# The gate behind the second dense weights, multiplied on TensorE instead of VectorE

## The chip, the core and the metric

The kernel runs on one core of a Trainium2 chip. The metric is the device time of one execution in microseconds (us); the kernel before has a median of 937.81 us in three runs (935.88 to 937.83).

## What is computed

Three layers follow one another. The first is a linear attention with a decaying state, over 4 sequences of 768 tokens and 8 heads of 48. Its output, 3072 rows of 384, goes through a dense layer (384 to 2048 and back) and then through a layer of 8 experts, in which each token goes to one expert by its logits, 384 tokens to each.

```python
for t in range(S):                                   # attention
    cur = np.einsum('bhd,bhe->bhde', u[None] * kt, vt)
    y[:, :, t] = np.einsum('bhd,bhde->bhe', rt, state + cur)
    state = wt[:, :, :, None] * state + np.einsum('bhd,bhe->bhde', kt, vt)

h = x @ w_in                                         # dense layer
g = h * (1.0 / (1.0 + np.exp(-1.702 * h)))
x = g @ w_out

logits = x @ w_gate                                  # experts: best (token, expert) pairs first
h = np.maximum(x[mask] @ w1[e], 0.0)
out[mask] = h @ w2[e]
```

For a block of tokens the logits are `(g @ w_out) @ w_gate`, which is also `g @ (w_out @ w_gate)`. The product of the two weights, 2048 x 8, is what this change is about.

## The kernel before

The 3072 tokens are cut into 8 blocks of 384 (`NB`), and the 2048 inner columns of the dense layer into 16 groups of 128 (`NFS`, index f). All weights and activations are held as a high and a low float32r part, so that a product takes three matmuls: high by high, high by low, low by high. `Ffn.g1` (line 1001) makes a group of g for a block in nine matmuls of 384 columns; `Ffn.part` (line 1029) multiplies it by the output weights into three accumulators of 128 tokens (`acc`).

The weights of the dense layer come as 64-bit numbers in 16 chunks, by turns one of `w_in` (two groups f) and one of `w_out` (two groups f). `split64` turns each into its two parts with steps on ScalarE, VectorE and GpSimd; the last step of a chunk is line 699, after which the plan sets `wdone[("in", i)]` or `wdone[("out", i)]`. `rhs2(f, part)` is the 128 x 384 piece of the output weights for group f. Meanwhile 24 `unit`s compute the attention, three for a block, with VectorE, GpSimd, ScalarE and small TensorE products.

The order of instructions on each engine is written by a small planner, `Issue` (line 60), when the program is built. It keeps a planned time `t` of TensorE and the planned time to which each other engine is busy. Chains (Python generators) are added with a rank; `pump` advances every chain whose time has come, lower ranks first. A step that yields `("T", d)` moves TensorE's time by d. `until(cond)` lets planned time go on in steps of 0.1 us until the condition holds, and issues in each step one `spin`: a matmul of the identity by itself (line 638), which computes nothing that is used. Three PSUM banks named `s1` are shared by the chains (`bank`).

The main loop runs over `seq`: half of block 0, block 1, the rest of block 0, then blocks 2 to 7, a g1 and, two places later, its g2. After a block's last g2 its rows x2 are stored, and `logits` (line 1073) multiplies them by the gate on VectorE, eight products with a sum for each 128 tokens.

The last block has no time for that, so its logits are made from g itself: `thin_logits` multiplies g by `wogp`, the high and low part of `wog` = `w_out @ w_gate`. `wog` is made by `wog_steps`, a chain of rank 5, the last rank. It starts when `gate_weights` has loaded the gate, spread over all partitions (`wgB`), after the last output chunk is split. For each f GpSimd adds the two parts of the weights (line 1137), and VectorE makes for each of the 8 experts a product with a sum along the row (line 1141, into `wog[:, f, e]`). At its end `todo[1] = 1` is set. Before the last block's first g1 the main loop waits for two things:

```python
if blk not in ffn:
    sc.until(lambda: xdone.get(blk) == NU)
    if blk == NBLK - 1:
        sc.until(lambda: todo[1])
```

After the last block come the router (eight rounds of a search on the logits) and the experts.

Of the kernel before, what the change touches and what calls it, by code (L numbers as in the profile page):

```python
# [8 lines left out]
F32 = mybir.dt.float32  # L9
F32R = mybir.dt.float32r  # L10
# [5 lines left out]
AF = mybir.ActivationFunctionType  # L16
OP = mybir.AluOpType
# [19 lines left out]
def dram(ap, off, dims):  # L37
    return bass.AP(tensor=ap.tensor, offset=ap.offset + off, ap=dims)
# [427 lines left out]
def kernel(ctx, tc, r, k, v, w, rk, u, us, w_in, w_out, w_gate, w1, w2, out):  # L466
    nc = tc.nc
    V, A, P, T = nc.vector, nc.scalar, nc.gpsimd, nc.tensor
    H, D = u.shape
    B, NC = r.shape[:2]  # L470
    Dm = H * D
# [3 lines left out]
    E, NC3 = w1.shape[:2]  # L475
# [3 lines left out]
    KT = Dm // 128  # L479
# [8 lines left out]
    NCVA, NCVB, NCVC = 3, 2, 3  # L488
# [18 lines left out]
    consts = ctx.enter_context(tc.tile_pool(name="consts", bufs=1))  # L507
# [6 lines left out]
    s1p = st1.enter_context(tc.tile_pool(name="s1p", bufs=1))  # L514
# [4 lines left out]
    sc = Issue()  # L519
    sc.nc = nc  # L520
    R = {n: Ring(m) for n, m in (("s1", 3), ("g1", 2), ("Q", 1), ("Fw", 1), ("At", 1),
                                 ("kn", 1), ("y", 1), ("g", 2), ("gh", 3), ("cva", NCVA), ("cvb", NCVB), ("cvc", NCVC),
                                 ("xa", 1), ("xb", 1), ("wk", 32), ("hold", NHOLD))}

    def wait(*names):
        while not all(R[n].ok() for n in names):
            yield 0.1

    def bank(shape=(128, 512)):
        yield from wait("s1")  # L530
        i = R["s1"].new()
        return psum.tile(list(shape), F32, name="s1", bufs=3), lambda: R["s1"].free(i)
# [82 lines left out]
    ident = consts.tile([128, 128], F32, name="ident")  # L615
    dif = cv.tile([128, 128], F32, name="cva", bufs=NCVA)
    P.iota(dif, pattern=[[1, 128]], base=0, channel_multiplier=-1, allow_small_or_imprecise_dtypes=True)
    V.tensor_scalar(ident, dif, 0.0, None, op0=OP.is_equal)  # L618
    later = s1p.tile([128, 128], U8, name="later")
    V.tensor_scalar(later, dif, 0.0, None, op0=OP.is_gt)  # L620
    lead = s1p.tile([R2, HP * PW + 1], U8, name="lead")
# [20 lines left out]
    Whi, Wlo, Wring, wdone = {}, {}, {}, set()  # L642
# [68 lines left out]
    def rhs2(f, part):  # L711
        return (Whi, Wlo)[part]["out", f // 2][:, (f % 2) * Dm:(f % 2 + 1) * Dm]
# [358 lines left out]
    wgB, scr = [], []  # L1071
# [57 lines left out]
    wog = consts.tile([128, NFS, E], F32, name="wog")  # L1129
    wogp = consts.tile([128, NFS * 2 * E + 128], F32R, name="wogp")  # L1130

    def wog_steps():
        while not wgB:
            yield 0.5
        for f in range(NFS):
            a = scr[0][:, 1]
            P.tensor_tensor(a, rhs2(f, 0).bitcast(F32), rhs2(f, 1).bitcast(F32), op=OP.add)  # L1137
            yield (("P", 1.0),)
            for e in range(E):
                yield from sc.room("V", 0.4)  # L1140
                V.scalar_tensor_tensor(scr[0][:, 0], a, 1.0,  # L1141
                                       wgB[e // 4][:, (e % 4) * Dm:(e % 4 + 1) * Dm],
                                       op0=OP.mult, op1=OP.mult, accum_out=wog[:, f, e:e + 1])
                yield (("V", 0.47),)
        hi, lo = (wogp[:, :NFS * 2 * E].rearrange("p (f x e) -> p f x e", f=NFS, x=2)[:, :, x]
                  for x in range(2))
        A.activation(hi, wog, AF.Copy)
        V.tensor_tensor(lo, wog, hi.bitcast(F32), op=OP.subtract)
        todo[1] = 1
# [52 lines left out]
    def thin_logits(f, ps):  # L1202
# [3 lines left out]
        for i in range(2):  # L1206
# [4 lines left out]
    start = [begin[un // NU] - LEAD[min(un // NU, 3)] + PACE[min(un // NU, 3)] * (un % NU)  # L1211
             for un in range(NUNIT)]
    slot = [-1]
    split64()
    for un in range(NUNIT):
        sc.add(unit(un) if un < NU else paced(un), 1 if un < NU else URANK)
    sc.add(gate_weights(), 3)
    sc.add(wog_steps(), 5)
    sc.add(get_part(), 2)
    sc.spin = spin  # L1220
    sc.until(lambda: xdone.get(0) == NU)
    ffn = {}
    for s in range(len(seq) + 2):
# [4 lines left out]
        if s < len(seq):  # L1228
            blk, f = seq[s]
# [13 lines left out]
        else:  # L1243
            if f2 == 0:
                last = ffn[b2]
                g_ = bank()
                try:
                    next(g_)
                except StopIteration as e:
                    ps, done = e.value  # L1250
# [188 lines left out]
    for s in range(E * NF3 + 2):  # L1439
        at[0] = s  # L1440
        i, f = divmod(s, NF3)
# [72 lines left out]
```

## Time and profile before

| | |
|---|---|
| median of 3 runs | 937.81 us |
| the profiled execution: time, span from first to last instruction | 941.33 us, 939.6 us |
| TensorE matmuls busy | 882.1 us (94%) |
| TensorE weight loads busy | 834.0 us (89%) |
| VectorE busy | 682.2 us (73%) |
| ScalarE busy | 350.9 us (37%) |
| GpSimd busy | 314.0 us (33%) |
| mean granted TensorE clock | 0.947 |

In the rows PE is TensorE's matmuls, PEld its weight loads, DVE VectorE, ACT ScalarE, POOL GpSimd. L1141 is line 1141. PEclk is the share of the full TensorE clock that was granted. A busy share says that an engine executes something, and not that the result is used: the spins of line 638 count as busy. Some of the time in which TensorE waits is therefore seen as spins and some as idle time.

### The profile page before, as it was taken

The numbers are of one execution on the slowest core, as the hardware profiler recorded it, in microseconds if no ns is written. First come the engines' busy times: TensorE is split into PE (matmuls) and PEld (weight loads), VectorE is DVE, ScalarE is ACT, GpSimd is POOL, SyncE is SP. The second block draws the span as 40 slices with busy tenths as digits, with TensorE's granted clock in tenths as the row PEclk, the third lists the DMA queues.
The fourth block names the chain that finished last, engine by engine and source line by source line (L and its number), as shares of the span: only waits on it lengthen the run. The fifth ranks groups of instructions, "written<-read, shape, count | busy, mean of one in ns | idle before, by whom it ended". The sixth has DMA issues, their size and how long they took to land.

```text
span 939.6 us, 18095 instructions
## 1 busy us (share of the span) xinstructions
PE 882.1 (94%) x6867; PEld 834.0 (89%) x6867; DVE 682.2 (73%) x1791; ACT 350.9 (37%) x632; POOL 314.0 (33%) x319
## 2 busy tenths in 40 slices
PE   6977997999999999999999979989999989999995
PEld 5766996899999999999999979979889889899995
DVE  8699699799979789799797783666676776653210
ACT  1433553332333333333323034024554643657521
POOL 4477346512232324233223101021333423346311
PEclk8779999899999999999999999978898998899998
DMA  8526432423313222133210000058787977969900
GB/s 262 160 85 190 143 110 95 143 85 96 98 51 96 73 75 82 50 97 97 63 54 5 2 25 1 18 151 187 190 241 154 275 207 155 259 186 268 245 26 26
DMA packets 48504, 113.37 MB, mean 121 GB/s; under 512 B 7616, under 2 KB 13600, under 8 KB 48416
## 3 DMA queue, kind: packets, MB, share of 16 engines
q1 hardware_dynamic: 31680, 70.51, 23.8%
q0 software_dynamic: 12288, 34.61, 17.5%
q10 hardware_dynamic: 4448, 7.08, 2.2%
q8 instruction: 54, 0.88, 0.4%
q14 instruction: 34, 0.28, 0.1%
HBM read 75.95 MB, written 10.03 MB: 91 GB/s over the span
## 4 chain that ended last, share of the span: by engine, by line
PE 62%; DVE 20%; issue 9%; DMA 3%; POOL 2%; ACT 2%; ACTq 0%; DVEq 0%; POOLq 0%
PE g L1001 24%; PE acc L1029 22%; PE s L393 5%; DVE cvb L1078 3%; DVE cvb L1141 3%; PE s L920 2%; PE s L913 2%; DVE Q L765 2%; DVE gl L1053 2%; PE s L836 2%; DVE cvc L681 2%; PE acc L638 1%; DVE cvc L678 1%; PE s L453 1%; DMA hold<-in_w 1%
## 5 line engine op out<-in xcount | busy, mean ns | idle before, releaser
L1029 PE MATMUL acc<-wk,gh 128*128 128x384 f32 x1080 | 282.0, 341 | 0.3 <-ACT cva L1406 0.3
L1029 PEld LDWEIGHTS acc<-wk,gh 128*128 128x128 f32 x1080 | 196.5, 191 | 1.5 <-ACT cva L1406 0.6
L1029 PE MATMUL acc<-wk,gl 128*128 128x384 f32 x540 | 183.1, 339 | 0.0
L1001 PE MATMUL g<-xhb,wk 128*128 128x384 f32 x576 | 171.1, 350 | 11.0 <-DVE gl L1053 5.2
L1001 PE MATMUL g<-xha,wk 128*128 128x384 f32 x576 | 171.8, 350 | 6.9 <-DVE gl L1053 3.7
L1047 ACT ACTIVATE g<-g 128x384 f32<-128x384 f32 x128 | 60.8, 475 | 217.4 <-PE g L1001 195.4
L1001 PEld LDWEIGHTS g<-xhb,wk 128*128 128x128 f32 x576 | 108.8, 195 | 13.4 <-DVE gl L1053 5.6
L1001 PEld LDWEIGHTS g<-xha,wk 128*128 128x128 f32 x576 | 108.3, 193 | 10.7 <-DVE gl L1053 5.3
L1029 PEld LDWEIGHTS acc<-wk,gl 128*128 128x128 f32 x540 | 103.0, 191 | 0.0
L1001 PE MATMUL g<-xlb,wk 128*128 128x384 f32 x288 | 100.3, 348 | 0.0
L1001 PE MATMUL g<-xla,wk 128*128 128x384 f32 x288 | 99.4, 345 | 0.0
L1078 DVE SCALAR_TENSOR_TENSOR cvb<-cva,raw 128x384 f32<-128x384 f32 x168 | 95.6, 569 | 4.6 <-ACT cva L1117 1.5
L1053 DVE TENSOR_TENSOR gl<-g,gh 128x384 fp32r<-128x384 f32 x116 | 64.0, 551 | 39.3 <-ACT gh L1050 38.9
L1330 POOL DMA_DIRECT2D wk<-hold x64 | 57.6, 1045 | 85.3 <-ACT wk L1324 76.6
L1060 ACT ACTIVATE gh<-g 128x384 fp32r<-128x384 f32 x64 | 31.3, 489 | 129.0 <-PE g L1001 113.9
L1141 DVE SCALAR_TENSOR_TENSOR cvb<-cvb,raw 128x384 f32<-128x384 f32 x128 | 71.4, 557 | 10.8 <-POOL cvb L1137 5.1
L1063 DVE SCALAR_TENSOR_TENSOR gl<-g,gh 128x384 fp32r<-128x384 f32 x64 | 35.2, 552 | 60.7 <-ACT gh L1060 56.0
L793 POOL TENSOR_TENSOR S<-S,Q 48x192 f32<-48x192 f32 x40 | 49.4, 1235 | 88.6 <-DVE Q L765 87.1
L638 PE MATMUL acc<-ident 128*128 128x128 bf16 x842 | 60.1, 227 | 4.2 <-DVE ident L618 4.2
L638 PEld LDWEIGHTS <-ident 128*128 128x128 bf16 x842 | 51.4, 102 | 10.1 <-issue 5.1
L1050 ACT ACTIVATE gh<-g 128x384 fp32r<-128x384 f32 x116 | 56.9, 490 | 8.5 <-DVE cva L1112 3.2
L393 PEld LDWEIGHTS <-cvc 128*128 128x128 bf16 x840 | 53.3, 158 | 5.9 <-issue 2.6
(222 smaller groups left out, 1432.4 us busy)
## 6 DMA issues: line engine op xcount, KB each, us to landing
hold<-in_w SPq DMA_DIRECT2D x64, 384.0 KB
wk<-hold POOLq DMA_DIRECT2D x64, 384.0 KB
nat_m<-in_rk SPq DMA_DIRECT2D x20, 384.0 KB
raw<-in_w_in SPq DMA_DIRECT2D x8, 768.0 KB
raw<-in_w_out SPq DMA_DIRECT2D x8, 768.0 KB
nat_v<-in_v SPq DMA_DIRECT2D x22, 256.0 KB
nat_w<-in_w SPq DMA_DIRECT2D x22, 226.2 KB
nat_k<-in_k SPq DMA_DIRECT2D x22, 224.0 KB
```

The costliest lines, as they stand in the source:

```text
L393: nc.tensor.matmul(ps[:, :E], G[j], oh[:, j], start=(j == 0), stop=(j == NJ - 1))
L638: T.matmul(warm[0][:, Dm:], i16, i16, start=warm[1], stop=False, skip_group_check=True)
L793: P.tensor_tensor(h_, h_, Q[64 * s:64 * s + D, 1:HP * PW:PW, None].to_broadcast([D, HP, D]), op=OP.mult)
L1001: T.matmul(p, self.l1(kt, f, a), (self.xh, self.xl)[b_][:, kt], start=(kt == 0 and n == 0), stop=(kt == KT - 1 and n == 2))
L1029: T.matmul(self.acc[tt], gs[a][:, tt * C:(tt + 1) * C], self.r2(f, b_), start=(f in self.cuts and n == 0), stop=(end and n == 2))
L1047: A.activation(p, p, AF.Gelu_apprx_sigmoid)
L1050: A.activation(gh, p, AF.Copy)
L1053: V.tensor_tensor(gl, p, gh.bitcast(F32), op=OP.subtract)
L1063: V.scalar_tensor_tensor(gl, p, 0.0, gh.bitcast(F32), op0=OP.max, op1=OP.subtract)
L1078: V.scalar_tensor_tensor(scr[0][:, 0], x2, 1.0, wgB[e // 4][:, (e % 4) * Dm:(e % 4 + 1) * Dm], op0=OP.mult, op1=OP.mult, accum_out=router. ...
L1141: V.scalar_tensor_tensor(scr[0][:, 0], a, 1.0, wgB[e // 4][:, (e % 4) * Dm:(e % 4 + 1) * Dm], op0=OP.mult, op1=OP.mult, accum_out=wog[:, f ...
L1330: P.dma_start(out=Wlo[key].bitcast(F32), in_=raw, accum_op=OP.add)
```

## The change

`wog_steps` is written anew. It no longer waits for the whole of the gate on all partitions. When the first output chunk is split it loads the gate as 8 rows of 384 (`wg8`), and TensorE turns it into three pieces of 128 x 8 (`wgT`). Then, for each f, as soon as its output chunk is split: six matmuls, whose stationary operands are the 128 x 128 pieces of the high and the low weights and whose moving operand is a float32r identity (`identr`), give the transposed sum of the two parts in a PSUM bank; ScalarE copies it to `wT`; three matmuls, `wT` by `wgT`, give the 128 x 8 piece of `wog`, which ScalarE copies. `wT` has one buffer with a ring of its own. The rank stays 5, `todo[1]` is set at the end as before, and `wgB` is still loaded for `logits`. GpSimd's addition and VectorE's eight products per f are gone.

```diff
-                                 ("kn", 1), ("y", 1), ("g", 2), ("gh", 3), ("cva", NCVA), ("cvb", NCVB), ("cvc", NCVC),
+                                 ("kn", 1), ("y", 1), ("wT", 1), ("g", 2), ("gh", 3), ("cva", NCVA), ("cvb", NCVB), ("cvc", NCVC),
...
+    identr = s1p.tile([128, 128], F32R, name="identr")
+    V.tensor_scalar(identr, dif, 0.0, None, op0=OP.is_equal)
...
+    wg8 = consts.tile([E, Dm], F32, name="wg8")
+    wgT = consts.tile([128, KT, E], F32, name="wgT")
+
     def wog_steps():
-        while not wgB:
+
+        while ("out", 0) not in wdone:
             yield 0.5
+        nc.scalar.dma_start(wg8, dram(w_gate, 0, [[Dm, E], [1, Dm]]))
+        yield 3.0
+        ps, done = yield from bank()
+        for kt in range(KT):
+            T.transpose(ps[:, kt * E:(kt + 1) * E], wg8[:, kt * 128:(kt + 1) * 128], ident[:E, :E])
+        A.activation(wgT, ps[:, :KT * E].rearrange("p (k e) -> p k e", k=KT), AF.Copy)
+        done()
+        yield (("T", 0.2), ("A", 0.2))
         for f in range(NFS):
-            a = scr[0][:, 1]
-            P.tensor_tensor(a, rhs2(f, 0).bitcast(F32), rhs2(f, 1).bitcast(F32), op=OP.add)
-            yield (("P", 1.0),)
-            for e in range(E):
-                yield from sc.room("V", 0.4)
-                V.scalar_tensor_tensor(scr[0][:, 0], a, 1.0,
-                                       wgB[e // 4][:, (e % 4) * Dm:(e % 4 + 1) * Dm],
-                                       op0=OP.mult, op1=OP.mult, accum_out=wog[:, f, e:e + 1])
-                yield (("V", 0.47),)
+            while ("out", f // 2) not in wdone:
+                yield 0.5
+            yield from wait("wT")
+            ps, done = yield from bank()
+            for kt in range(KT):
+                for n in range(2):
+                    T.matmul(ps[:, kt * 128:(kt + 1) * 128], rhs2(f, n)[:, kt * 128:(kt + 1) * 128], identr,
+                             start=(n == 0), stop=(n == 1))
+            yield (("T", 0.9),)
+            yield from sc.room("A", 0.4)
+            i = R["wT"].new()
+            wT = s1p.tile([128, KT * 128], F32, name="wT")
+            A.activation(wT, ps[:, :KT * 128], AF.Copy)
+            done()
+            yield (("A", 0.5),)
+            ps, done = yield from bank()
+            for kt in range(KT):
+                T.matmul(ps[:, :E], wT[:, kt * 128:(kt + 1) * 128], wgT[:, kt], start=(kt == 0),
+                         stop=(kt == KT - 1))
+            R["wT"].free(i)
+            A.activation(wog[:, f], ps[:, :E], AF.Copy)
+            done()
+            yield (("T", 0.4), ("A", 0.2))
```

## Rows read from the trace of the kernel before

**Rows 1.** The page's first line.

```profile
span 939.6 us, 18095 instructions
```

**Rows 2.** Windows: stretch and its length, busy time (count) by engine, clock, DMA, GB/s.

```profile
45.00:103.00 58.00, 46.90 (x426) 42.76 (x425) 53.15 (x63) 22.19 (x38) 38.92 (x26) 0.88 0.42 132
103.00:150.00 47.00, 42.52 (x250) 40.58 (x248) 41.00 (x49) 23.99 (x42) 22.55 (x13) 1.00 0.37 120
150.00:172.20 22.20, 17.49 (x190) 16.37 (x190) 18.72 (x22) 4.71 (x7) 15.82 (x12) 0.77 0.41 125
172.20:519.80 347.60, 346.66 (x2505) 334.60 (x2501) 298.23 (x756) 115.46 (x242) 99.58 (x99) 1.00 0.25 75
519.80:538.00 18.20, 18.20 (x327) 18.20 (x327) 13.96 (x50) 0.00 (x0) 2.98 (x3) 1.00 0.01 2
538.00:549.80 11.80, 6.57 (x41) 6.25 (x38) 9.08 (x32) 1.86 (x5) 1.01 (x1) 0.99 0.01 1
549.80:552.80 3.00, 3.00 (x9) 3.00 (x10) 2.50 (x8) 1.47 (x4) 0.00 (x0) 0.50 0.37 131
```

The columns of busy time are PE, PEld, DVE, ACT and POOL, in this order.

**Rows 3.** Windows of line 638 (the spins): stretch, length, PE and PEld busy, clock, DMA.

```profile
45.00:103.00 58.00, 8.61 (x134) 7.59 (x134) 0.88 0.42 132
103.00:150.00 47.00, 0.00 (x0) 0.00 (x0) 1.00 0.37 120
150.00:172.20 22.20, 4.31 (x71) 4.05 (x71) 0.77 0.41 125
```

**Rows 4.** Waits of PE from 165 to 560 us: total, times, longest.

```profile
PE g L1001 <- DVE gl L1053: 5.4, 2, 5.2
```

**Rows 5.** Timeline around the last block's start: start, us, what, idle time before.

```profile
519.79 18.43 PE L638 MATMUL acc<-ident 128*128 128x128 bf16 x327
...
547.91 0.31 ACT L1147 ACTIVATE wogp<-wog 128x128 fp32r<-128x128 f32 x1 [28.49 <-DVE cvb L1141]
...
549.76 0.69 PE L1001 MATMUL g<-xhb,wk 128*128 128x384 f32 x1 [5.23 <-DVE gl L1053]
```

**Rows 6.** Groups from 165 to 560 us: busy us, mean ns of one, idle before.

```profile
L1141 DVE SCALAR_TENSOR_TENSOR cvb<-cvb,raw 128x384 f32<-128x384 f32 x128 | 71.4, 557 | 10.8 <-POOL cvb L1137 5.1 <-DMA raw<-in_w_gate 2.6
L1050 ACT ACTIVATE gh<-g 128x384 fp32r<-128x384 f32 x92 | 45.1, 490 | 7.5 <-DVE cva L1112 3.2 <-ACT cva L1117 2.4
L1141 DVE DVE_READ_ACCUMULATOR cvb<-cvb,raw 128x1 f32 x128 | 10.4, 81 | 0.0
```

**Rows 7.** Line 977 from 460 to 560 us: duration, first and last start.

```profile
L977 POOL TENSOR_TENSOR xlb<-y,xhb x3: 1014/1048/1271, 480.6 to 513.2; 128x384 fp32r<-128x384 f32 x3
```

**Rows 8.** Timeline of PE from 281 us on, at the full clock.

```profile
281.24 0.60 PE L855 MATMUL s<-ident,nat_k 112*128 112x112 f32 x4
281.62 0.59 PE L1029 MATMUL acc<-wk,gh 128*128 128x384 f32 x2
...
282.75 1.05 PE L913 MATMUL s<-nat_r,S 112*128 112x128 f32 x8
283.74 0.44 PE L920 MATMUL s<-At,nat_v 128*64 128x128 f32 x4
```

**Rows 9.** The chain that ended last, from 300 us on: one of nine matmuls.

```profile
303.74 1.56 PE acc L1029 x9
```

**Rows 10.** Windows of line 699: stretch, length, DVE and POOL busy (count), clock, DMA.

```profile
30.00:103.00 73.00, 2.09 (x2) 13.82 (x6) 0.86 0.44 136
103.00:150.00 47.00, 0.00 (x0) 10.60 (x5) 1.00 0.37 120
150.00:172.20 22.20, 1.68 (x1) 4.44 (x2) 0.77 0.41 125
```

**Rows 11.** Waits of DVE from 103 to 172 us: total, times, longest.

```profile
DVE gl L1053 <- ACT gh L1050: 3.0, 2, 1.8
```

**Rows 12.** The chain that ended last, from 160 us on: the gate's transfer.

```profile
168.29 5.03 DMA raw<-in_w_gate
```

## The prediction

> **What bounds the kernel now.** I read the profile in this order: the span and its shares, then the stretches, then what TensorE executes in each, then its waits. The profiled execution has a span of 939.6 us [rows 1]; the run around it took 941.33 us and the median of the runs shown is 937.81 us. So I sum on the span and take 1.8 us off at the end.
>
> The stretches [rows 2] show three regimes. From 172.2 to 519.8 us TensorE is busy 346.66 of 347.60 us at the full clock: it is the bound, and what VectorE does there costs nothing as long as TensorE doesn't wait for it. From 45 to 172.2 us TensorE is not full (46.90 of 58.00, 42.52 of 47.00, 17.49 of 22.20) and VectorE has about as much to do (53.15, 41.00, 18.72); this is the stage that splits the incoming weights. Then the busy share misleads: 519.8 to 538.0 us reads 18.20 of 18.20 busy, yet it is no work. The timeline [rows 5] shows 327 matmuls of line 638 there, 18.43 us from 519.79. Line 638 is `spin`, which multiplies the identity by itself while the plan waits. So a busy TensorE has to be corrected by the spins, which the windows of line 638 give [rows 3]: 8.61 us from 45 to 103, none from 103 to 150, 4.31 us from 150 to 172.2.
>
> What is waited for at 519.8 us is in the code: before the last block's first g1 the loop runs `sc.until(lambda: todo[1])`, and `todo[1]` is set at the end of `wog_steps`. The trace agrees: ScalarE's first step on `wog` starts at 547.91 us after 28.49 us of idleness that VectorE's line 1141 ended [rows 5]. The plan gave VectorE too little time per step, so TensorE, having spun, runs a little and then stands idle 5.23 us until 549.76 us for a `gl` that lies behind the rest of line 1141 in VectorE's queue [rows 5]. That one wait is 5.2 of the 5.4 us that the main loop's g1 waited for VectorE from 165 to 560 us [rows 4]. After the idle stretch it runs 3.00 us at a granted clock of 0.50 [rows 2], the lower of its two levels.
>
> **What the change removes.** 128 products on VectorE of 557 ns and 128 accumulator reads of 81 ns [rows 6], 82 us, with GpSimd's 16 additions ahead of them. In the TensorE-bound stretch that is worth nothing. Its worth lies at the end: spinning 519.79 to 538.03, 18.2 us; the idle 5.2 us; half of 3.0 us at the half clock, 1.5 us. Sum 24.9 us, if `todo[1]` is set before 519.8 and nothing else is late there. What is late next? The last block's x: its last piece (line 977, `xlb`) starts at 513.2 us and takes about 1 us [rows 7], 5.6 us ahead of the wait. Then TensorE is simply continuous.
>
> By the Trainium skill ("Trainium Kernel Development and Optimization", Best Practices) one should judge TensorE by MFU and by the busy share of LDWEIGHTS instead of matmul busy time. Here LDWEIGHTS is 18.20 of 18.20 us [rows 2] while nothing is computed, so the row decides against that rule.
>
> **What it adds.** Per f, six matmuls (three column groups, high and low part, moving `identr`), one ScalarE copy of 128x384, three products with `wgT` of eight columns, and a small ScalarE copy. The trace has no float32r matmul with 128 moving columns, so I bound it. A one-instruction transpose of 112 columns takes (281.62 - 281.24) / 4 = 0.095 us, a full-precision product (two instructions each) (283.74 - 282.75) / 8 = 0.124 us per instruction [rows 8]; float32r with 384 columns takes 1.56 / 9 = 0.173 us in one instruction [rows 9]. One instruction it will be, as there: I take 0.11, so 6 x 0.11 = 0.66 us; ends 6 x 0.095 = 0.57 and, if it went as two passes, 6 x 0.248 = 1.49 us. The three `wgT` products are plain float32: 6 instructions x 0.124 = 0.74 us. Together 1.40 us per f (ends 1.31 and 2.23), 22.4 us for 16. That is nearly as much as the gain, so all depends on where it lands.
>
> The Trainium skill ("FP8 and Floating Point Precision", TensorE Precision Notes) says true FP32 takes four passes. The rows have two instructions per product, as long as two loads. By the page the `wgT` part would be 1.49 us per f and the sum 34.4 us.
>
> It lands early, since f starts when its output chunk is split. The windows of line 699, where each split ends, count 8, 5 and 3 splits [rows 10], every second one an output chunk; the fourth output chunk ends at the edge of the first window, so I count f = 0 to 5 to the first stretch, 6 to 11 to the second, 12 and 13 to the third, and 14 and 15 after it. TensorE's free time (idle plus spins [rows 2, 3]) is 11.1 + 8.6 = 19.7, 4.5, and 4.7 + 4.3 = 9.0 us. Added: 8.4 into 19.7, hidden; 8.4 into 4.5, 3.9 carried on; 2.8 + 3.9 = 6.7 into 9.0, hidden; and f = 14, 15 at the start of the full stretch, 2.8 us on the path. The free time need not lie where the new work does: TensorE may reach a unit's products late and VectorE then waits for them. Against much of that speaks that from 103 to 172 us VectorE waited for TensorE's line (gl, through ScalarE) only 3.0 us [rows 11]: TensorE has been the one that waits, and a later arrival waits less. I put a quarter of the 11.2 us of the second and third stretch on the path, 2.8 us. So 5.6 us are given back.
>
> Smaller edits: ScalarE gains 16 copies of 490 ns [rows 6] and 16 tiny ones, in a stage where it is mostly idle; between copy and `wgT` products TensorE could stand up to 0.5 us, unless main-loop matmuls lie between, as the plan wants: nothing, bound 8 us. The three transposes wait in TensorE's queue for the transfer of `wg8`, and everything behind them too; the gate's broadcast took 5.03 us [rows 12] and is far larger, so I take zero (bound 2 us; spins lie there). One bank of three is held for about a microsecond per f: units that need all three start later, part of the quarter. One more VectorE comparison of 128x128 at the start: less than one 557 ns step, none taken.
>
> **Sum.** 939.6 - 24.9 + 5.6 = 920.3 us of span; minus 1.8, 918.5 us.
>
> **Rivals.** (1) Everything but the last chunk is absorbed and the 24.9 us come whole: 913 to 915.5 us. For it: 33.2 us free against 19.6. Chance 0.13. (2) The 128-column products cost two passes, 2.23 us per f: second stretch 13.4 into 4.5, carry 8.9; third 4.5 + 8.9 = 13.4 into 9.0, 4.4 left; 4.5 for the last two; a quarter of the 13.5 us that the two stretches do absorb, and some waits for the copy, 5: about 14 us back, 927 us. Chance 0.12. (3) Slower: the weight stage becomes TensorE's. Each f puts its two passes and its wait for the copy, in order, ahead of the units' products, so that splits and units queue behind: 16 x (2.23 + 0.5) = 43.7 us against 24.9 gives 956.6 us. It decides from 24.9 / 16 = 1.56 us exposed per f. Against it: the free time above. Chance 0.05. (4) It doesn't do what it says: something else holds the last block at 519.8 for the same 18.2 us, say the plan's date for its x; then 6.7 - 5.6 = 1.1 us remain, 936.7 us. Against it [rows 7]. Chance 0.03. (5) The spun stretch counts as full: then only 6.7 us can be won and 22.4 us of matmuls come on top, 953.5 us; rows 5 speak plainly against it, 0.01. By the page on LDWEIGHTS above it would be the likely one.
>
> **How the numbers follow.** The forecast, 914 to 924 us with 918.5 as its middle, has 0.66. The range from 913 (nothing given back) to 927 takes in rivals 1 and most of 2, about 0.85 of the chance. A change of 0.2% (1.9 us) is about what a measurement of this kernel tells from none. Faster by more: 0.66 + 0.13 + 0.12 = 0.91; same, rival 4: 0.03; slower, 0.06.
>
> **What would show it.** Right: no long run of line 638 before the last block, no 5 us wait after it, `wogp` written by about 180 us, and TensorE's solid stretch starting some 3 to 6 us later than 172.2. The first six matmuls of an f start to start: 0.11 us or 0.25. Wrong: a spin run that stays (then look at the last block's x), TensorE waiting for `wT`, or the first solid stretch beginning after 187 us.

## The result, and the profile after

Four runs of the changed kernel have a median of 923.96 us (922.10 to 927.46), beside 937.27 us for four runs of the kernel before: a ratio of 0.985, 95% interval 0.983 to 0.988. The kernel is 13.3 us faster; forecast were 19.3. The profiled execution, with a span of 925.8 us, is the slowest of the four.

First the stretches, with the columns of [rows 2], for the kernel after:

```profile
45.00:103.00 58.00, 49.17 (x443) 45.45 (x441) 53.07 (x61) 25.41 (x52) 41.86 (x27) 0.88 0.42 132
103.00:150.00 47.00, 44.22 (x278) 43.56 (x278) 42.30 (x43) 26.61 (x52) 24.49 (x13) 1.00 0.38 118
150.00:172.20 22.20, 20.08 (x123) 19.09 (x123) 18.79 (x21) 5.46 (x12) 11.99 (x8) 0.69 0.15 41
172.20:519.80 347.60, 345.10 (x2533) 331.73 (x2532) 251.80 (x583) 115.59 (x242) 78.79 (x89) 1.00 0.27 80
519.80:538.00 18.20, 18.20 (x107) 18.20 (x106) 4.17 (x10) 6.91 (x16) 1.02 (x1) 1.00 0.04 12
```

The stretch 519.8 to 538.0 still reads 18.20 of 18.20, but with 107 matmuls in place of 327: now it is work. The windows of the spins (line 640 here; length, PE and PEld busy, clock, DMA) show it, and the timeline of TensorE shows the last block's first g1 (line 1003) directly behind the g2 (line 1031) ahead of it:

```profile
45.00:103.00 58.00, 5.84 (x76) 4.63 (x76) 0.88 0.42 132
150.00:172.20 22.20, 0.00 (x0) 0.00 (x0) 0.69 0.15 41
519.00:531.00 12.00, 0.00 (x0) 0.00 (x0) 1.00 0.01 3
```

```profile
530.16 0.33 PE L1031 MATMUL acc<-wk,gl 128*128 128x384 f32 x1
530.33 0.33 PE L1003 MATMUL g<-xhb,wk 128*128 128x384 f32 x1
```

In the kernel before, this same g1 would have stood at 519.79 us, where the spins begin [rows 5]. So the last block no longer waits, but it comes 10.5 us later. Its x is not late, as [rows 7] promised. The question for the runs is where those 10.5 us come from, and what of them the products cost.

What the new steps take is read from one timeline row of each (start, us, what, idle time before; the executions of a row overlap) and, for the count, from the view of line 1156:

```profile
173.96 0.78 PE L1156 MATMUL s<-identr,wk 128*128 128x128 f32 x6
174.57 0.39 PE L1003 MATMUL g<-xha,wk 128*128 128x384 f32 x1
...
188.01 0.73 PE L1167 MATMUL s<-wgT,wT 128*128 128x8 f32 x6
188.59 0.59 PE L1031 MATMUL acc<-wk,gh 128*128 128x384 f32 x2
```

```profile
L1156 PE MATMUL s<-identr,wk x96: 221/275/415, 48.9 to 182.6; 128*128 128x128 f32 x96
```

From start to the next start the six transposing matmuls take 174.57 - 173.96 = 0.61 us, 0.10 each, and the three products with `wgT`, two instructions each, 188.59 - 188.01 = 0.58 us. That is 1.19 us per f where the granted clock was 1.00, as it was from 172.2 us on.

### The profile page after: what moved, and what is told of

Read it like the earlier page. It is cut to its first block, busy times and chain, and to the rows that moved or that the text cites. A ratio compares the mean times of both kernels' runs of the same rounds, so it can differ in the third digit from the quotient of the medians.

```text
span 925.8 us, 17341 instructions
## 1 busy us (share of the span) xinstructions
PE 878.2 (95%) x6606; PEld 830.0 (90%) x6606; DVE 617.6 (67%) x1535; ACT 361.5 (39%) x665; POOL 291.2 (31%) x304
## 4 chain that ended last, share of the span: by engine, by line
PE 68%; DVE 15%; issue 8%; DMA 3%; POOL 3%; ACT 1%; ACTq 0%; DVEq 0%; POOLq 0%
PE g L1003 25%; PE acc L1031 24%; PE s L393 5%; DVE cvb L1080 4%; PE s L922 3%; PE s L838 2%; PE s L915 2%; DVE gl L1055 1%; PE s L453 1%; DVE Q L767 1%; DVE cvc L680 1%; DMA cvb<-x2d,idx 1%; DVE cvb L689 1%; PE s L1393 1%; PE acc L640 1%
## 5 line engine op out<-in xcount | busy, mean ns | idle before, releaser
L1003 PE MATMUL g<-xha,wk 128*128 128x384 f32 x576 | 174.1, 352 | 5.2 <-DVE gl L1055 2.4
L1080 DVE SCALAR_TENSOR_TENSOR cvb<-cva,raw 128x384 f32<-128x384 f32 x168 | 97.8, 582 | 11.0 <-ACT cva L1119 7.8
L1065 DVE SCALAR_TENSOR_TENSOR gl<-g,gh 128x384 fp32r<-128x384 f32 x64 | 35.1, 551 | 60.9 <-ACT gh L1062 60.9
L795 POOL TENSOR_TENSOR S<-S,Q 48x192 f32<-48x192 f32 x40 | 43.9, 1098 | 92.0 <-DVE Q L767 85.4
L1003 PEld LDWEIGHTS g<-xla,wk 128*128 128x128 f32 x288 | 56.3, 196 | 0.0
L1351 ACT ACTIVATE wk<-hold 128x768 fp32r<-128x768 f32 x64 | 53.5, 837 | 7.2 <-DMA hold<-in_w 7.2
L393 PE MATMUL s<-oh,cvc 128*128 128x8 bf16 x840 | 55.6, 201 | 0.2 <-DVE xlb L1404 0.2
```

What stands on the lines that cost most here:

```text
L393: nc.tensor.matmul(ps[:, :E], G[j], oh[:, j], start=(j == 0), stop=(j == NJ - 1))
L795: P.tensor_tensor(h_, h_, Q[64 * s:64 * s + D, 1:HP * PW:PW, None].to_broadcast([D, HP, D]), op=OP.mult)
L1003: T.matmul(p, self.l1(kt, f, a), (self.xh, self.xl)[b_][:, kt], start=(kt == 0 and n == 0), stop=(kt == KT - 1 and n == 2))
L1065: V.scalar_tensor_tensor(gl, p, 0.0, gh.bitcast(F32), op0=OP.max, op1=OP.subtract)
L1080: V.scalar_tensor_tensor(scr[0][:, 0], x2, 1.0, wgB[e // 4][:, (e % 4) * Dm:(e % 4 + 1) * Dm], op0=OP.mult, op1=OP.mult, accum_out=router. ...
L1351: A.activation(Whi[key], raw, AF.Copy)
```

## The experiments

All times are given as a ratio to the kernel before, which ran beside each kernel on the same chip; "us" behind a ratio is the ratio times 937.3 us. The changed kernel was timed once more among them. By "lag" I mean how much later than in `e_none` the last block's first g1 starts in the profiled execution; except in `e_late` it hardly changes from the first g1 of block 2 on, since TensorE is full from there. A lag is read from one execution of each kernel. The kernel before, which makes no f on TensorE, has by it 1.9 us (519.79 against 517.87), and the first profile of the changed kernel 12.5 where `e_after` has 10.9; so lags that differ by 2 us or less are not told apart. What follows behind that g1 takes 390.8 to 397.0 us in these executions, and so a time and a lag can differ by some us. The difference of two ratios is uncertain by 4 to 5 us to either side. What the expectations call theories are accounts of these same costs: the products' own time on TensorE, or the order and the waits that they bring.

| kernel | what of f TensorE makes | ratio (95% interval) | us | lag, us |
|---|---|---|---|---|
| e_none | nothing | 0.974 (0.971 to 0.977) | 912.8 | 0 |
| e_f0_5 | f = 0 to 5 | 0.973 (0.971 to 0.975) | 911.8 | 2.6 |
| e_f6_13 | f = 6 to 13 | 0.973 (0.970 to 0.975) | 911.6 | 2.0 |
| e_f14_15 | f = 14, 15 | 0.978 (0.975 to 0.981) | 916.5 | 2.3 |
| e_f0_13 | f = 0 to 13 | 0.977 (0.974 to 0.981) | 915.8 | 5.4 |
| e_f6_15 | f = 6 to 15 | 0.978 (0.974 to 0.981) | 916.3 | 5.4 |
| e_after | all (the changed kernel) | 0.984 (0.981 to 0.988) | 922.5 | 10.9 |
| e_thin | all, a third or less of the matmuls | 0.982 (0.978 to 0.985) | 920.1 | 4.6 |
| e_lead | all, units planned earlier | 0.982 (0.979 to 0.986) | 920.7 | 10.9 |
| e_one_bank | all, one bank instead of two | 0.990 (0.987 to 0.994) | 928.1 | 14.5 |
| e_late | all, behind the last chunk | 0.997 (0.995 to 1.000) | 934.8 | 27.0 |
| e_split6 | f = 0 to 5; VectorE the rest | 0.972 (0.971 to 0.974) | 911.4 | 1.4 |

### The wait alone: e_none

`wog` is filled by one copy from weights that have already come, so the last block's logits are other numbers; all steps for an f are left out.

```diff
-        nc.scalar.dma_start(wg8, dram(w_gate, 0, [[Dm, E], [1, Dm]]))
...
-        for f in range(NFS):
...
+        A.activation(wog.rearrange("p f e -> p (f e)"), rhs2(0, 0)[:, :NFS * E].bitcast(F32), AF.Copy)
```

> Leaves the product of the two weights out altogether: wog is filled, by one ScalarE copy, with 128 columns of the output weights, so the last block's logits are those of other weights; nothing waits for it. It measures what the waiting before the last block was worth. All theories: before less 24.9 us, 912.4 us. If it is not under 917, the 24.9 us were counted too high and the products are not what gives the gain back.

Measured 0.974: 24.5 us from the kernel before. The removal is worth what the sum said (24.9), and nothing else is late behind it. So the changed kernel gives back 0.9842 - 0.9739 = 0.0103, 9.7 us (uncertain by 4.6 to either side), where the forecast had 5.6. All that follows is about these 9.7 us.

### The changed kernel again, and its own matmuls thinned: e_after, e_thin

`e_after` has no edit. `e_thin` keeps every step, its copies and its planned time, but makes one of the six and one of the three matmuls:

```diff
-            for kt in range(KT):
-                for n in range(2):
-                    T.matmul(ps[:, kt * 128:(kt + 1) * 128], rhs2(f, n)[:, kt * 128:(kt + 1) * 128], identr,
-                             start=(n == 0), stop=(n == 1))
+            T.matmul(ps[:, :128], rhs2(f, 0)[:, :128], identr, start=True, stop=True)
...
-            for kt in range(KT):
-                T.matmul(ps[:, :E], wT[:, kt * 128:(kt + 1) * 128], wgT[:, kt], start=(kt == 0),
-                         stop=(kt == KT - 1))
+            T.matmul(ps[:, :E], wT[:, :128], wgT[:, 0], start=True, stop=True)
```

> The changed kernel again, on the chip of its variants: 922 to 925 us by every theory.

> The changed kernel with its plan untouched (the same steps, the same planned times, banks and copies), but of the six matmuls per f only one is made and of the three products only one, so that wog is another one. TensorE's own time for it falls from 1.2 us per f to about 0.3. Theory 1 (what is given back is TensorE's own time for these matmuls): 914 to 916 us. Theory 2 (it is the new waits, TensorE standing in order for a bank of s1 that a unit's score products hold until VectorE has read them): as the changed kernel, 922 to 924 us. Theory 3 (the plan's order has shifted the units by the planned 1.3 us per f): 922 to 924 us too.

With over two thirds of the matmuls gone, 0.0103 above `e_none` becomes 0.0077: only 2.4 us come back in time, 6.3 in lag, and the 920.1 us lie between what the theories expected. The intervals overlap. The matmuls that are left still take 0.16 and 0.13 us per f (from start to next start at 175 and 181 us), 4.6 us for sixteen, as much as the lag that stays. So the share of the products' own time is not settled, and a part of the cost that does not hang on how long the matmuls take is possible by the times and not shown. Such a part would be waits or order, and the waits come first. These are the waits of TensorE from 45 to 215 us in the kernel after (total, times, longest), and its timeline:

```profile
PE s L1167 <- DVE wk L845: 5.7, 1, 5.7
PE g L1003 <- DVE gl L1055: 3.7, 3, 2.4
PE s L1167 <- DVE At L845: 2.5, 2, 2.1
```

```profile
60.70 1.45 PE L1167 MATMUL s<-wgT,wT 128*128 128x8 f32 x6 [5.71 <-DVE wk L845]
...
161.55 1.45 PE L1167 MATMUL s<-wgT,wT 128*128 128x8 f32 x6 [2.12 <-DVE At L845]
...
177.82 0.83 PE L1167 MATMUL s<-wgT,wT 128*128 128x8 f32 x6 [0.35 <-DVE At L845]
```

Line 845 is the select with which VectorE reads a unit's score products out of their bank. The plan counts the bank as free once that select is issued, and gives it to `wog_steps` as the second bank of an f. On the chip TensorE, which takes its instructions in order, then stands until VectorE has read. In `e_after` the middle one of these waits is 3.99 us. VectorE's timeline tells why it takes so long: the select waits behind the splits' steps, such as line 690.

```profile
157.73 1.16 PE L838 MATMUL s<-nat_r,nat_k 48*128 48x128 f32 x16
158.82 0.60 PE L857 MATMUL s<-ident,nat_k 112*128 112x112 f32 x4
```

```profile
159.59 1.27 DVE L690 SCALAR_TENSOR_TENSOR cvb<-raw,cvb 128x768 f32<-128x768 uint32 x1
160.78 1.33 DVE L845 COPY_PREDICATED At<-later,s 128x512 f32<-128x512 uint8 x2
```

This stand is not new, however. The kernel before stands for the same select (there line 843) with the products that the unit makes next, first below, and so does `e_none`, whose waits from 45 to 215 us have the second line:

```profile
166.61 2.07 PE L913 MATMUL s<-nat_r,S 112*128 112x128 f32 x8 [4.59 <-DVE At L843]
```

```profile
PE s L915 <- DVE At L845: 5.9, 2, 4.5
```

In all TensorE stands for line 845 in this view 8.3 us in `e_none`, 10.7 in `e_after`, and 12.8 in `e_f0_5`, which is as fast as `e_none` (below). So the stand has moved to another line, and that it is what the change costs is not shown.

### Holding one bank through the copy: e_one_bank

If the second bank is what TensorE stands for, an f could keep its first bank and put the products behind the transposed weights in it.

```diff
             A.activation(wT, ps[:, :KT * 128], AF.Copy)
-            done()
...
-            ps, done = yield from bank()
+            o_ = ps[:, KT * 128:KT * 128 + E]
```

> The three products go into the free columns of the bank that the six matmuls filled, so a second bank per f isn't asked for. Theory 1: unchanged, 922 to 924 us. Theory 2: the 8.2 us of idleness before line 1167 (5.71 at 55 us, 2.12 at 159 us, 0.35 at 177 us) is gone and 3 to 8 us are won: 916 to 920 us. Theory 3: unchanged or a little slower, as a bank is held longer.

It is slower than the changed kernel by 0.990 - 0.984 = 0.006, 5.6 us, where the theory of the bank wanted 3 to 8 us won. The waits go to other places; this is the same view, of this kernel:

```profile
PE s L1156 <- DVE wk L845: 3.4, 2, 3.0
PE g L1003 <- POOL wk L701: 3.3, 1, 3.3
PE s L1156 <- DVE At L845: 3.0, 2, 2.7
```

The first bank is now the one that VectorE has yet to read, and holding it through the copy keeps the units from it: the sixth unit has its score products at 94.62 us, in the kernel after at 85.51. Three banks are scarce, in whichever way they are given out.

### Part by part: e_f0_5, e_f6_13, e_f14_15, and f = 0 to 5 with VectorE for the rest: e_split6

The first three fill `wog` as `e_none` does, and then make only some f, so again the logits of the last block are other numbers. The edit of `e_f0_5` stands here; `e_f6_13` has `range(6, 14)` and `e_f14_15` has `range(14, 16)`.

```diff
-        for f in range(NFS):
+        for f in range(6):
```

> Only f = 0 to 5 are made on TensorE, those that come while TensorE has most free time; the other rows of wog stay filled with columns of the output weights, so this leaves ten sixteenths of the product out. The prediction had this part hidden: as without any product, 913 us. If the plan's shift of the units costs wherever it comes, 916 or more.

> Only f = 6 to 13 are made on TensorE, the rest of wog stays filled with columns of the output weights. The prediction had 2.8 us of it on the path: 916 us. If these eight groups are what the first sum got wrong, they cost 5 to 7 us: 918 to 920 us.

> Only f = 14 and 15 are made on TensorE, the rest of wog stays filled with columns of the output weights. They come when TensorE is full: 2 x 1.2 = 2.4 us plus the 0.35 us that they wait for a bank, 915.5 to 916 us. If it is 913 they are hidden after all; if 918 or more, waits or order come with them.

`e_f0_5` and `e_f6_13` can't be told from `e_none`, though 916 us had been expected of the second; `e_f14_15` is 3.7 us above it, with overlapping intervals. Their lags are 2.0 to 2.6 us each, hardly more than that of the kernel before. Alone, each part fits as far as these runs can tell. The whole doesn't: it costs 9.7 us, 8.2 more than the parts together, and 10.9 in lag against 6.9. The uncertainty of that difference is about 8 us too, so that the parts cost more together than alone is likely and not shown.

`e_split6` computes everything: TensorE makes f = 0 to 5, and a second chain, which starts when `wgB` has come, makes f = 6 to 15 with the steps of the kernel before.

```diff
+    NTE = 6
...
-        for f in range(NFS):
+        for f in range(NTE):
...
+        todo[1] = 0.5
+
+    def wog_rows():
+        while not wgB or not todo[1]:
+            yield 0.5
+        for f in range(NTE, NFS):
...
+    sc.add(wog_rows(), 5)
...
-                    sc.until(lambda: todo[1])
+                    sc.until(lambda: todo[1] == 1)
```

> Nothing is left out: f = 0 to 5 on TensorE as they come, f = 6 to 15 on VectorE as before the change, where it has time beside the TensorE-bound stretch. Before the change VectorE had made about 11 of 16 by 519.8 us, so ten are ready in time and the last block waits for nothing. If the early groups are hidden, 913 to 915 us; if they cost 3 us, 916; if VectorE's ten aren't ready when the plan asks, a rest of the spins stays, some 3 to 6 us more.

0.972 (0.971 to 0.974): faster than both kernels, by 26 us and by about 11, and equal to `e_none`. Ten f fit on VectorE ahead of the last block where sixteen did not. ScalarE's first step on the whole `wog` and the last block's first g1 in its timeline:

```profile
506.32 0.30 ACT L1192 ACTIVATE wogp<-wog 128x128 fp32r<-128x128 f32 x1
```

```profile
519.27 0.33 PE L1003 MATMUL g<-xhb,wk 128*128 128x384 f32 x1
```

The margin is 13 us, where the kernel before spun 18.2 us [rows 5], while TensorE has 6 f to place in the roomiest stretch.

### What adds up: e_f0_13, e_f6_15

> f = 0 to 13 are made on TensorE, the last two rows of wog stay filled with columns of the output weights. f = 0 to 5 alone and f = 6 to 13 alone cost nothing that could be measured (912.9 and 912.7 us). Theory A, each stretch takes in its own part and the cost is that of the last chunk: 913 us. Theory B, lateness adds up: the first six leave TensorE 3 to 4 us late at 103 us, the next eight come on top, the units of block 2 start later since their start hangs on TensorE's place in the main loop, and their products fall behind the last split: 918 to 920 us.

> f = 6 to 15 are made on TensorE, the first six rows of wog stay filled with columns of the output weights. Theory A: as f = 14 and 15 alone, 915 to 918 us. Theory B: the lateness of f = 6 to 13 is made good by the last split (TensorE's main loop was 2 us ahead there), so the last two add their 2.4 us and waits: 915 to 918 us too. 920 or more would say that the first six have no part in what is given back.

The edit is that of `e_f0_5`, with `range(14)` and `range(6, 16)`. Fourteen f cost 0.9771 - 0.9739 = 0.0032, 3.0 us (lag 5.4), between what theories A and B expected; ten f, the last two among them, 3.5 us (lag 5.4). So f = 14 and 15 cost 3.7 us alone and 0.9842 - 0.9771 = 0.0071, 6.7 us, on top of the other fourteen; in lag 2.3 and 5.5. The two times are uncertain by more than 4 us each, so the lags alone set them apart, and not by much. The windows at the start of the full stretch show a part of that (columns as in [rows 2]), first of `e_f0_13`, then of `e_after`:

```profile
172.20:205.00 32.80, 32.80 (x263) 31.71 (x262) 25.09 (x62) 12.21 (x26) 6.88 (x9) 1.00 0.50 165
```

```profile
172.20:205.00 32.80, 31.77 (x263) 30.12 (x262) 20.54 (x46) 11.32 (x27) 6.36 (x8) 1.00 0.46 152
```

Without the last two f TensorE is full from 172.2 us. With them it stands 1.03 us in this window and 0.63 behind it: 0.35 for a bank, the rest for a `gl` that VectorE makes late. Their own products are 2 x 1.19 = 2.4 us. Together 4.1 of the 5.5 us of lag; the rest is less than the difference between two executions of one kernel.

The stretches ahead of 172.2 us tell how the free time was used. Windows of `e_none`, then its spins, then the same of `e_after` (which has spins in the first stretch alone):

```profile
45.00:103.00 58.00, 45.06 (x439) 41.07 (x438) 53.97 (x65) 24.12 (x44) 39.10 (x26) 0.94 0.41 132
103.00:150.00 47.00, 42.39 (x247) 40.28 (x247) 41.69 (x49) 23.71 (x42) 24.37 (x16) 0.99 0.40 132
150.00:172.20 22.20, 17.74 (x192) 16.58 (x192) 16.78 (x19) 3.80 (x6) 12.36 (x8) 0.79 0.44 137
```

```profile
45.00:103.00 58.00, 8.52 (x134) 7.54 (x134) 0.94 0.41 132
150.00:172.20 22.20, 4.59 (x71) 4.17 (x71) 0.79 0.44 137
```

```profile
45.00:103.00 58.00, 48.37 (x441) 45.27 (x440) 51.88 (x61) 25.68 (x51) 40.34 (x26) 0.91 0.42 132
103.00:150.00 47.00, 44.19 (x275) 43.59 (x274) 42.47 (x43) 25.67 (x51) 24.47 (x13) 0.98 0.35 119
150.00:172.20 22.20, 18.21 (x132) 17.46 (x132) 19.62 (x23) 6.24 (x13) 11.53 (x8) 0.81 0.14 45
```

```profile
45.00:103.00 58.00, 5.83 (x76) 4.63 (x76) 0.91 0.42 132
```

`e_none` has idle 12.94 + 4.61 + 4.46 and spins 8.52 + 4.59, 35.1 us free. `e_after` has 9.63 + 2.81 + 3.99 and 5.83, 22.3 us, left. So 12.8 us of the free time were used, for fourteen f that need at least 14 x 1.19 = 16.7 us: some 4 us of the main loop's work were pushed out of these stretches while 22.3 us stayed free. Free time that lies where TensorE waits for a split or a unit is no place for work that arrives elsewhere.

### Whether the units' later start is the cause: e_lead

In the changed kernel the last two units of block 2 have their score products (line 838) at 157.73 and 175.77 us, in `e_none` at 143.7 and 158.0. One account was that TensorE's planned time, moved on by the new steps, lets units start too late. This edit starts those of block 2 earlier in the plan:

```diff
-    LEAD = (0, 9, 15, 16)
+    LEAD = (0, 9, 18, 16)
```

> The changed kernel, nothing left out, but the units of block 2 start three places of the main loop earlier (LEAD of that block 18 in place of 15), about as much as they came too late. Theory B: unit 7's products are back in TensorE's free time before the last split, 3 to 6 us won: 916 to 919 us. Theory A, or if it is TensorE's own time: no change, 922 us; slower if the earlier units delay the splits.

The later of the two units moves to 163.75 us, but the last split now ends at 178.9 us instead of 170.2 in `e_after`, and the lag stays 10.9; 0.982 against 0.984 is no difference that the intervals show. VectorE has steps in both, and one of them is late: the units' start alone is not the cause.

### Nothing hidden: e_late

All sixteen f wait for the gate on all partitions, so that they come behind the last output chunk.

```diff
-            while ("out", f // 2) not in wdone:
+            while not wgB:
```

> The changed kernel, nothing left out, but the first f waits until all chunks are split and the gate is loaded, so all 16 groups lie in the stretch in which TensorE is full. Nothing is hidden: 913 + 16 x 1.2 = 932 us, some 1 to 3 us more for waits. It measures what the hidden part is worth: 932 - 922 = 10 us of 19. If it comes near 922, nothing was hidden before.

0.997, 22 us above `e_none` (uncertain by 3.9 to either side; 27.0 in lag), for 16 x 1.19 = 19.0 us of products. So a price that is fully on the path is about its own size plus some waits, and hiding is worth about 12 of these 22 us: the products are hidden by a little over half.

## Why the prediction was right or wrong

**The gain.** Forecast 24.9 us, measured 24.5 by `e_none`. Each part of it is seen: no spins before the last block, no wait of 5 us for `gl` behind it, `wog` ready 330 us ahead (`wogp` is written at 189.5 us; I had said 180). The Trainium skill ("Trainium Kernel Development and Optimization", Best Practices) would have one judge how near a kernel comes to its roofline by MFU and by the busy share of weight loads, not of matmuls. That share reads 18.20 of 18.20 in this stretch before [rows 2] and after, though 18.2 us of it were won: here the count of useful instructions decided and the share did not. One sign failed: TensorE's solid stretch does not start 3 to 6 us after 172.2. In the kernel after TensorE is busy 9.30 of the 9.30 us from 162.9 to 172.2 us, without a spin; the lateness lies in what is still to be done there, such as a unit's products at 175.77 us. Rivals 4 and 5 fall. Rival 3 wanted 43.7 us given back; with all sixteen f on the path `e_late` gives back 22, still less than the gain.

**The price of an f.** Forecast 1.40 us, measured 1.19: 0.61 against 0.66 for the first six, and 0.58 against 0.74 for the products with `wgT`. So the float32r matmuls take 0.10 us each and not the 0.25 of rival 2, which falls in its mechanism, though its 927 us were nearer than its price. The Trainium skill ("FP8 and Floating Point Precision", TensorE Precision Notes) gives four passes for true FP32. My estimate of 1.49 us per f from that page did not come true, but products of 8 columns don't tell how many passes an instruction makes, so no run here decides on the page. By the price alone the kernel would have come out faster than forecast: with 1.19 the prediction's own way of adding gives back 2.4 for the last two and 2.4 for the quarter, 4.8 us. That the forecast's 5.6 came nearer to the 9.7 is luck.

**The last chunk: the term that was mis-sized.** I put f = 14 and 15 on the path with their own 2.8 us. On top of the other fourteen they cost 6.7 us in time and 5.5 in lag. I took them as work appended to a full stretch; but TensorE stands 1.7 us there for a bank and for `gl`, which it does not without them. My account is that TensorE enters that stretch late already, and that behind the last split VectorE has the late units, the selects that free the banks and the main loop's `gl` all at once. That they cost less alone (3.7 us, lag 2.3) fits it, but the intervals of the two times overlap, so that it is the sum of lateness and not the two f is not shown.

**The quarter.** 2.8 us on the path for f = 6 to 13, nothing for f = 0 to 5. Measured for both together 3.0 us in time, uncertain by 4.5, and 5.4 in lag. As a size it is not contradicted. The reasoning, by which f = 6 to 13 cost it and f = 0 to 5 nothing, found no support: each part alone costs nothing that can be measured, and their lags of 2.6 and 2.0 us are alike. Rival 1 (all absorbed) would hold for either half; for both it is the lag of 5.4 that speaks against it, and the time does not.

**The bank.** I gave the copy a wait of nothing, with a bound of 8 us, and the bank a part of the quarter. For the copy it was nearly nothing (0.2 us in the kernel after). The wait that came is another: ahead of the products with `wgT` TensorE stands for a bank that VectorE has not yet read, 5.71 us at 55 us (it costs nothing by `e_f0_5`), 2.12 or 3.99 at 160. I named who is queued behind the copy and did not ask who holds the bank that the products go into. But as the kernel before stood 4.59 us for the same select, this wait is not shown to be a part of the 9.7 us. The transfer of `wg8`, which I put at zero with a bound of 2 us, held TensorE up 2.65 us in `e_after` and 2.44 in `e_f0_5`, which is no slower than `e_none`.

**VectorE's readiness.** I argued from [rows 11] that VectorE seldom waits for TensorE, so that a later arrival would wait less. That holds from 103 to 150 us, where TensorE's idle time falls from 4.61 to 2.81. But [rows 11] are of the main loop's `gl`, and what came late are the units' products. For these VectorE now waits itself; here are its waits from 103 to 215 us, first of `e_none`, then of `e_after`:

```profile
DVE At L845 <- PE s L838: 1.5, 1, 1.5
```

```profile
DVE At L845 <- PE s L838: 3.2, 2, 1.9
DVE S L886 <- PE s L874: 2.3, 1, 2.3
```

So lateness is handed back: VectorE stands for late units, and units that come earlier cost the splits instead, as in `e_lead`, where the last split ends 8.7 us later.

**The sum.** The forecast of 918.5 us lies 5.5 us below the median, which is at the edge of the forecast's 914 to 924 us. The term that was mis-sized is what is given back: 9.7 us by `e_none` and `e_after` against 5.6, which makes 4.1 of the 5.5 us; the others come from the difference between the two comparisons, 0.985 and 0.984. By the times alone 5.6 is still inside the uncertainty of 4.6; the lags of 10.9 and 12.5 in the two profiles of the changed kernel speak for the larger figure. How the 9.7 us divide between TensorE's own time and waits stays open: `e_thin` says 2.4 us by time and 6.3 by lag, and the intervals allow both.

## What to carry to other kernels

Work moved into an engine's free time was paid in part here, though the free time was about twice as large: count only the free time that lies where the new work arrives, and test the parts together, since each may seem to fit alone. If a late step only has to be ready in time, move so much of it that it is ready, and leave the rest where it costs nothing: six of sixteen parts here gave the whole gain, all sixteen gave a little over half of it. Where a plan frees a buffer when its reader is issued, an engine that works in order stands for that reader with everything behind it; before you call such a stand the cost of a change, look for it in the kernel before.

## What had not been expected of the hardware

A float32r matmul with a stationary 128 x 128 and 128 moving columns is followed by the next after 0.10 us, hardly more than the 0.095 us of a transpose with 112 columns [rows 8]; and a plain product with only 8 columns takes 0.097 us per instruction, so that its price is hardly that of its columns. The mean granted clock from 150 to 172.2 us was 0.69 in the execution of the changed kernel with 2.12 us of standing ahead of line 1167, 0.81 in another of the same kernel with 3.99 us of it, and 0.77 before [rows 2]: in this stretch, in which the spins of the kernel before are gone, it differs from one execution to the next by as much as between the kernels.
